# A rewritten opening: two dummies ahead of the data, other line sums, another order of the first steps

## The chip, the cores and the metric

The kernel runs on one core of a Trainium2 chip. The metric is device time in microseconds of one execution. The kernel before takes 1026.65 us (median of 3 runs, 1025.84 to 1027.16).

## The reference

Attention over a pooled key/value image, followed by a gated feed-forward network (FFN). There are 4 images (B), 12288 query rows (N) each, 128 channels (C).

```
kv_pool = kv.reshape(B, 96, 4, 8, 4, C).mean(axis=(2, 4))      # 4x4 pooling: 768 keys
k = v   = kv_pool.reshape(B, 768, C) @ w_sr
a       = softmax(q @ k.T / sqrt(C))
x       = (a @ v).reshape(B * N, C)
out     = (relu(x @ w_gate) * (x @ w_val)) @ w_out             # hidden width 1536
```

Inputs and output are fp32.

## The kernel before, in words

**Tiles.** The 49152 query rows are cut into 96 tiles of 512 rows (`T`). Four tiles are a group (`GRP`) that is loaded together. The 768 keys of an image are six chunks of 128 (`NJC`), the FFN's hidden width is 12 blocks of 128 (`NFB`). For each tile the kernel computes scores, exponentials, the weighted sum x of the values, the FFN's two projections, their gated product and the output projection. The division by the sum of the exponentials is put off to the output, where its square is applied, since the gated product is of second degree in x.

**The order of the work** is written out by hand. Each engine takes its instructions strictly in the order in which the words of a list emit them. A steady tile runs the words of `STEADY`, the last tiles those of `DRAIN` and `LAST`. Ahead of that stands one long list, `OPENING`: it covers the load, pooling and projection of image 0, tiles 0 to 3 through the attention, tiles 0 to 2 through the FFN's projections, the output projections of tiles 0 and 1, and the scores of tiles 4 and 5. A word may carry `@n`, the PSUM bank that its result is to use; a product into a bank waits until the bank's last reader is done.

**The words of OPENING** (the function `open_step` turns them into instructions):

- `Tj.d` turns line d of chunk j: four 128x128 fp32 transposes on TensorE, accumulated in one bank, so that the turn also adds the four pixels of a line (`turn_add`, L280, instructions at L285). A chunk's pooling is a sum over 4 lines of 4 pixels.
- `aj`, `bj`, `cj` add lines of a chunk elementwise on VectorE or GpSimd before any turn (`sum_lines`; `SUMS` says which lines, "s" being the sum so far). `pj` adds the sum's pixels 0,1 to 2,3, and `rj` those two to one (`sum_pixels`). `Tj.p` then turns two blocks, `Tj.r` one block, in place of four for each line.
- `kvTj` copies the turned chunk out of PSUM (`turned`), `pjj` projects it (`project_chunk`, L299), `keyj` keeps the keys, `vtj` transposes them to values (L310), `valj` keeps those.
- `casti` converts a query tile to fp16, `qti` transposes it on TensorE (L205), `qTi` copies it out. For tiles 4 and 5, `qT` is a DMA transpose instead.
- `Sk.j` is the score product of tile k with chunk j (L359), `Ek.j` its exponential on ScalarE (L362), `Vk.j` the product with the values (L437), `xTk` the copy of x. `U` sums the exponentials of chunks with a product by ones (L455), `R` turns those sums into the output's scales.
- `vk.f`, `gk.f`, `ok.f` are the FFN products (L478, L489, L519), `yk.f` copies a v product out of PSUM (by default on ScalarE), `hk.f` multiplies it with the gate on VectorE (L497). `sk.n`, `ek.n` are the scores and exponentials in the steady form.
- `gate`, `W`, `wo`, `ql`, `qd`, `qn`, `tq`, `k` issue DMAs: the FFN's weights, query tiles 4 and 5, the second half of query group 1, later groups.
- `F256` is one dummy product, 256 columns wide.

`ENGINES` names the engine of the words that have a choice (a ScalarE, v VectorE, p GpSimd).

**Loads.** Lines of two chunks are one DMA of 512 KB (`kv_load`, L242). In order of issue on the sync queue, with lines 1 and 3 of the first pair on ScalarE's queue: the four lines of chunks 0 and 1; `w_sr`; query tiles 0 and 1 as one DMA; line 0 of chunks 2 and 3; query tiles 2 and 3; lines 1 to 3 of chunks 2 and 3; the four lines of chunks 4 and 5 (`kv_line`).

**Dummies.** `fill(3)` (L639, instructions at L635) issues three products of 512 columns on the identity matrix before any data is needed. Being fp32, each runs as two passes. They write the bank that the first turn uses next.

Of the kernel before, what the change touches and what calls it, by code (L numbers as in the profile page):

```python
# [9 lines left out]
FP32 = mybir.dt.float32  # L10
# [6 lines left out]
def kernel(  # L17
# [27 lines left out]
    r = 4  # L45
# [18 lines left out]
    assert NFB == 2 * NJC and NST % GRP == 0 and W // r == 8 and HC == 64  # L64

    ENGINES = dict(word.split(":") for word in """
        kvT0:v cast1:a cast0:p kvT1:v key0:v key1:a val0:v qT1:a qT0:v val1:a cast2:v cast3:a
        qT2:v a2:v a3:v p2:v qT3:v b3:p c3:v kvT2:a p3:v key2:a kvT3:a val2:v a5:v a4:v key3:a
        p5:v b4:v r5:v c4:v val3:a kvT5:a p4:v key5:a kvT4:v key4:v val5:a val4:v cast4:p xT2:v
        xT3:v y2.0:v cast5:p y2.3:a y2.1:v y2.2:a y2.5:a y2.6:a xT1:a y2.4:a y1.5:a y1.4:a xT0:a  # L70
        y1.9:a y1.6:a y1.1:a y1.7:a y1.3:a y0.11:a y1.2:a y0.7:v y1.11:a y1.0:a y0.4:a y1.8:a
        y1.10:a y0.2:a y0.8:v y0.5:a y0.10:a y0.0:a y0.3:a y2.11:a y0.9:a y0.1:a y0.6:a y2.8:v
        y2.10:a y2.7:a y2.9:a
    """.split())
    OPENING = """
        T0.1@0 T1.1@1 T0.0 T1.0 F256 T0.3 T0.2 T1.2 kvT0 T1.3 cast1 cast0 pj0@0 kvT1 key0 pj1@1
        vt0@0 qt1@2 key1 val0 qt0@3 qT1 vt1@1 qT0 val1 S1.0@0 S1.1@1 E1.0 S0.1@2 cast2 S0.0@3
        cast3 qt2@4 V1.0@0 qT2 E0.1 qt3@5 a2 S2.1@4 E1.1 S2.0@2 V0.1@6 E2.1 a3 V1.1 E2.0 V2.1@1
        p2 T2.2@4 E0.0 qT3 b3 T2.p S3.0@2 V0.0 E3.0 T2.3 S3.1@3 c3 kvT2 V3.0@2 E3.1 V2.0 pj2@4 p3
        V3.1 key2 T3.p@3 S2.2@4 kvT3 vt2@5 S1.2@7 E2.2 val2 pj3@3 gate2.1 a5 W0 S3.2@5 E1.2 V2.2  # L80
        a4 S0.2@4 key3 E3.2 V1.2 S3.3@3 p5 S2.3@7 E0.2 W1 ql4 ql5 T5.2@5 b4 E3.3 V3.2 vt3@4 V0.2
        r5 E2.3 T5.3 c4 wo val3 T5.r V3.3 kvT5 p4 S0.3@3 pj5@4 E0.3 T4.p@5 S1.3@7 key5 kvT4 V2.3
        E1.3 S3.5@3 pj4@4 E3.5 vt5@5 S2.5@7 key4 V0.3 val5 S2.4@4 E2.5 vt4@3 S3.4@5 val4 V3.5
        E2.4 V2.5 S0.4@3 E3.4 cast4 V2.4 S1.5@4 E0.4 xT2 V1.3 qT4 V3.4 E1.5 S1.4@5 xT3 V0.4 E1.4
        v2.0@1 qd1 v2.3@3 y2.0 v2.1@4 cast5 y2.3 v2.2@2 V1.5 y2.1 g2.0@5 y2.2 qd3 qT5 v2.5@1
        v2.6@3 h2.0 qd0 y2.5 g2.1@2 g2.5@4 V1.4 y2.6 qd2 h2.1 g2.2@1 v2.4@5 xT1 g2.3@3 h2.2
        g2.4@2 y2.4 S0.5@7 h2.3 v1.5@0 E0.5 v1.4@1 v1.9@5 h2.4 g1.5@3 y1.5 V0.5 U0.1.2.3.4.5@7
        h2.5 y1.4 xT0 h1.5 y1.9 v1.6@0 R g1.9@1 y1.6 v1.1@2 v1.7@3 h1.9 g1.7@4 y1.1 v1.3@0 g1.1@5
        tq1 y1.7 s4.0 h1.1 g1.6@1 y1.3 v0.11@2 g1.2@3 e4.0 h1.6 o1.5@5 o1.1 v1.2@0 h1.7 g1.4@1
        y0.11 s4.1 h1.4 y1.2 g1.3@4 v0.7@2 e4.1 o1.6 h1.3 qn1.3 g0.11@0 v1.11@1 o1.4 y0.7 y1.11  # L90
        v1.0@4 o1.3 h0.11 s4.2 y1.0 g1.0@1 e4.2 g1.8@2 h1.2 v0.4@0 v1.8@4 h1.0 o1.9 y0.4 g1.11@3
        s4.3 y1.8 h1.11 o1.0 v0.8@0 e4.3 k5 g0.7@1 h1.8 v1.10@3 o1.2 g0.4@4 h0.7 y1.10 v0.2@2
        o1.7 h0.4 y0.2 o1.11 v0.5@1 g0.10@3 y0.8 y0.5 g1.10@2 o1.8 g0.2@4 h1.10 v0.10@1 v0.0@0
        y0.10 s5.0 h0.2 o0.4@2 y0.0 o1.10 h0.10 g0.8@1 e5.0 v2.11@4 v0.3@0 oT1 o0.10 g0.9@3 y0.3
        o0.11 h0.8 g0.0@5 y2.11 o0.7 h0.0 g0.3@0 v0.9@1 v0.1@4 h0.3 y0.9 s5.1 o0.0 y0.1 v0.6@5
        h0.9 v2.10@0 e5.1 g2.6@1 g0.6@4 h2.6 o0.3 v2.8@3 y0.6 o0.2 y2.8 s5.2 y2.10 g2.9@1 v2.7@5
        h0.6 e5.2 g0.1@3 g2.7@0 o0.8 h0.1 g0.5@4 y2.7 s5.3 h0.5 v2.9@3 e5.3 g2.8@5 o0.9 h2.7
        g2.11@4 o0.5 y2.9 o0.6 h2.8 o0.1 g2.10@0 h2.9 h2.10 h2.11 oT0
    """.split()
    LAST = [f"{head}{n}" for n in range(NFB) for head in "ovygh"] + ["oT"]  # L100
    DRAIN = """
# [42 lines left out]
    def engine_of(name):  # L144
        return {"a": nc.scalar, "v": nc.vector, "p": nc.gpsimd}[ENGINES.get(name, "a")]

    def q_load(g):
        if not 0 <= g < NG:
            return
        b, n0 = divmod(g * GRP * T, N)  # L150
        q16 = work.tile([128, GRP * NS, C], FP16, tag="q16", bufs=2)
        rows = q[b, n0 : n0 + GRP * T, :]
        if g == NG - 1:
            nc.gpsimd.dma_start(q16, rows.rearrange("(p s) c -> p s c", p=128))
        else:
            rows = rows.rearrange("(i t j s) c -> j t i s c", i=GRP, t=32, s=NS)
            for j in range(4):
# [117 lines left out]
    def sum_pixels(name, chunk):  # L275
        s1 = sums.pop(chunk)
        pixels[chunk] = work.tile([128, 2, C], FP32, tag="kv_c2", bufs=2, name="kv_c2")
        add(name, pixels[chunk], s1[:, 0:2], s1[:, 2:4])

    def turn_add(chunk, lines):  # L280
        first = chunk not in kv_Ts
        if first:
            kv_Ts[chunk] = bank([128, 128])
        for i in range(lines.shape[1]):
            nc.tensor.matmul(  # L285
                kv_Ts[chunk], lines[:, i], ident, is_transpose=True,
                start=first and i == 0, stop=False, skip_group_check=True,
            )

    def turned(name, chunk):  # L290
        kvT = work.tile([128, 128], FP32, tag="kvT_chunk", bufs=3, name="kvT_chunk")
        copy_on(name, kvT, freed(kv_Ts[chunk]))
        kv_Ts[chunk] = kvT
# [3 lines left out]
    def project_chunk(jc):
        key_ps[jc] = bank([128, 128])
        nc.tensor.matmul(key_ps[jc], w_sr_f32, kv_Ts.pop(jc), start=True, stop=True)  # L299

    def keep_keys(name, jc):
        pr, engine = freed(key_ps.pop(jc)), engine_of(name)
        if engine is nc.scalar:
            nc.scalar.mul(kv16[:, 0, jc, 0:C], pr, 1.0 / (r * r))
        else:
            engine.tensor_scalar(kv16[:, 0, jc, 0:C], pr, 1.0 / (r * r), None, op0=ALU.mult)

    def turn_chunk_values(jc):
        value_ps[jc] = bank([128, 128], FP16)
        nc.tensor.transpose(value_ps[jc], kv16[:, 0, jc, 0:C], ident16)  # L310

    def keep_chunk_values(name, jc):
        copy_on(name, kv16[:, 0, jc, C : 2 * C], freed(value_ps.pop(jc)))
# [336 lines left out]
    def open_step(word):  # L650
# [59 lines left out]
        elif head == "gate":  # L710
            nc.gpsimd.tensor_copy(gate, line(2 * at[0], at[1])[:, 0, 0:1])
        elif head == "ql":
            q_load_tile(at[0])
        elif head == "wo":
            nc.gpsimd.dma_start(wo16, moe_w_out.rearrange("(fb f) c -> f fb c", f=128))
        elif head == "qd":
            q_tiles(1)
            rows = q[0, GRP * T : 2 * GRP * T, :].rearrange(
                "(i t j s) c -> j t i s c", i=GRP, t=32, s=NS
            )  # L720
            j = at[0]
# [148 lines left out]
```

## Time and profile before

| quantity | value |
|---|---|
| median of 3 runs | 1026.65 us |
| the profiled execution, its own time | 1026.18 us |
| its span in the trace | 1024.4 us |
| TensorE busy | 1017.8 us (99%) |
| ScalarE busy | 919.4 us (90%) |
| VectorE busy | 865.0 us (84%) |
| GpSimd busy | 523.4 us (51%) |
| data moved by DMA | 153.49 MB, mean 150 GB/s |

The profile is one execution on the chip. Its time includes 1.8 us around the span of the trace. A line of the trace's timeline gives the start, the duration, the engine (PE is TensorE's products, PEld its weight loads, DVE VectorE, ACT ScalarE, POOL GpSimd, SP the sync engine), the source line, the operation with output and input, the count of merged instructions, and in brackets the idle time before it with what ended it. Products overlap: the duration of one covers its latency, so the rate is read from start to start. Stretches are given in microseconds from the span's start.

### The profile page before, as it was taken

Reading aid. Unit: us, or ns where it says so; the run is one execution under the profiler, and the core shown is the slowest. Engines: PE = TensorE matmul, PEld = TensorE weight load, DVE = VectorE, ACT = ScalarE, POOL = GpSimd, SP = SyncE. Lnnn points to the kernel's source line nnn. Section 1 sums busy time; section 2 is a strip of 40 time slices with the busy share of each in tenths; the row PEclk is TensorE's granted clock in tenths of the full one; section 3 lists DMA queues with packets and bytes.
Section 4 is the critical chain, followed back from the end, with each engine's and each line's share of the span. In section 5 each row is a group of like instructions: output and inputs, shape, how many; then the busy total and the mean of one; then the engine's idle time right before and its main releaser. Section 6 shows DMA issues by size and latency. Waiting matters only on the chain.

```text
span 1024.4 us, 17497 instructions
## 1 busy us (share of the span) xinstructions
PE 1017.8 (99%) x5039; PEld 488.2 (48%) x5039; DVE 865.0 (84%) x1439; ACT 919.4 (90%) x1929; POOL 523.4 (51%) x1308
## 2 busy tenths in 40 slices
PE   9999999999999999999999999999999999999998
PEld 5444444444444444444444444444444444444445
DVE  3988888888888888888888888888888888888887
ACT  5999999999999999999999999999999999999986
POOL 2587857344347576544434856754334443443342
PEclk9999999999999999999999999999999999999999
DMA  9999999887898998869889899797686986876641
GB/s 318 149 188 158 180 209 145 164 137 126 133 200 156 188 198 152 142 119 144 132 131 199 164 186 206 136 143 134 119 137 105 148 129 119 129 124 115 108 83 42
DMA packets 475312, 153.49 MB, mean 150 GB/s; under 512 B 451536, under 2 KB 465360, under 8 KB 475216
## 3 DMA queue, kind: packets, MB, share of 16 engines
q1 hardware_dynamic: 453184, 126.08, 67.0%
q0 software_dynamic: 21600, 25.19, 16.1%
q10 hardware_dynamic: 432, 1.11, 0.3%
q8 instruction: 40, 0.66, 0.3%
q14 instruction: 56, 0.46, 0.1%
HBM read 53.94 MB, written 26.35 MB: 78 GB/s over the span
## 4 chain that ended last, share of the span: by engine, by line
PE 99%; ACT 0%; issue 0%; POOL 0%; DVE 0%; POOLq 0%
PE bank_ps L489 24%; PE bank_ps L478 24%; PE bank_ps L519 24%; PE wide_ps L378 12%; PE bank_ps L420 12%; PE bank_ps L503 1%; PE bank_ps L285 1%; PE bank_ps L635 1%; PE bank_ps L437 0%; PE bank_ps L359 0%; PE wide_ps L317 0%; ACT aT L362 0%; PE bank_ps L299 0%; PE bank_ps L455 0%; ACT qT L140 0%
## 5 line engine op out<-in xcount | busy, mean ns | idle before, releaser
L497 DVE SCALAR_TENSOR_TENSOR hT<-bank_ps,val 128x512 f16<-128x512 f32 x1152 | 728.0, 679 | 104.0 <-PE bank_ps L489 83.2
L140 ACT CAST val<-bank_ps 128x512 f16<-128x512 f32 x1147 | 628.0, 596 | 44.9 <-PE bank_ps L478 24.9
L478 PE MATMUL bank_ps<-xT,wv 128*128 128x512 f16 x1152 | 419.7, 379 | 0.0
L489 PE MATMUL bank_ps<-xT,wg 128*128 128x512 f16 x1152 | 376.5, 379 | 0.0
L519 PE MATMUL bank_ps<-hT,wo 128*128 128x512 f16 x1116 | 348.2, 379 | 0.0
L383 ACT ACTIVATE a<-wide_ps 128x768 f16<-128x768 f32 x368 | 302.1, 821 | 43.3 <-PE wide_ps L378 43.2
L378 PE MATMUL wide_ps<-kv,qT 128*128 128x512 f16 x736 | 179.7, 326 | 0.0
L420 PE MATMUL bank_ps<-aT,kv 128*128 128x512 f16 x552 | 178.8, 379 | 0.0
L519 PEld LDWEIGHTS <-wo 128*128 128x128 f16 x1116 | 109.2, 98 | 131.6
L489 PEld LDWEIGHTS <-wg 128*128 128x128 f16 x1152 | 112.7, 98 | 122.7
L532 POOL TENSOR_TENSOR o_sb<-o_t,scale 128x512 f32<-128x512 f32 x89 | 93.3, 1049 | 144.7 <-issue 127.2
L478 PEld LDWEIGHTS <-wv 128*128 128x128 f16 x1152 | 112.7, 98 | 105.1 <-issue 0.6
L404 POOL COPY scale<-square 32x8 f32<-32x8 f32 x736 | 141.8, 193 | 28.6
L397 POOL TENSOR_TENSOR square<-inverse 128x8 f32<-128x8 f32 x46 | 9.4, 203 | 256.2 <-DVE inverse L395 249.1
L800 POOL DMA_DIRECT2D out_dram<-o_sb x208 | 130.5, 630 | 16.1 <-POOL o_sb L532 13.0
L378 PEld LDWEIGHTS <-qT 128*128 128x128 f16 x736 | 72.0, 98 | 86.9 <-issue 0.2
L428 DVE CAST xT<-bank_ps 128x512 f16<-128x512 f32 x92 | 63.6, 691 | 32.1 <-PE bank_ps L420 32.1
L420 PEld LDWEIGHTS <-kv 128*128 128x128 f16 x552 | 54.0, 98 | 65.1
L383 ACT ACTIVATION_READ_ACCUMULATOR a<-wide_ps 128x1 f32 x368 | 76.0, 206 | 0.0
L527 DVE STREAM_TRANSPOSE o_t<-bank_ps 128x512 f32<-128x512 f32 x93 | 65.4, 703 | 0.1
L158 POOL DMA_DIRECT2D q<-in_q_dram x84 | 46.7, 572 | 0.6 <-ACT val L140 0.4
L252 POOL TENSOR_TENSOR s<-kv_in 128x512 f32<-128x512 f32 x36 | 45.2, 1284 | 0.7
(83 smaller groups left out, 208.0 us busy)
## 6 DMA issues: line engine op xcount, KB each, us to landing
kv_in<-in_kv_dram SPq DMA_DIRECT2D x42, 512.0 KB, 4.8
out_dram<-o_sb SPq DMA_DIRECT2D x177, 64.0 KB, 3.7
out_dram<-o_sb POOLq DMA_DIRECT2D x176, 64.0 KB, 4.3
q<-in_q_dram POOLq DMA_DIRECT2D x84, 128.0 KB, 6.3
aT<-a SPq DMA_TRANSPOSE x184, 4.6
kv_line<-in_kv_dram SPq DMA_DIRECT2D x4, 512.0 KB, 9.9
placed<-blocks SPq DMA_DIRECT2D x9, 128.0 KB, 2.2
kvT<-placed SPq DMA_DIRECT2D x36, 32.0 KB, 2.0
```

Of the source, the lines that this page charges most:

```text
L140: nc.scalar.copy(to, what)
L378: nc.tensor.matmul(s_ps[:, j0 * 128 : j1 * 128], qT, kv16[:, b, j0:j1, 0:C], start=True, stop=True)
L383: nc.scalar.activation(a16s[k][:, s, :], s_banks.pop(s)[:, 0:J], AF.Exp, scale=qk_scale, accum_out=a_sums[k // 2][:, k % 2, s : s + 1],)
L404: nc.gpsimd.tensor_copy(to[32 * b : 32 * (b + 1), :, :, j], squares[k // 2][32 * j : 32 * (j + 1)])
L420: nc.tensor.matmul(x_banks[k], kv16[:, k // NST, jc, C : 2 * C], aT[:, jc], start=first, stop=x_left[k] == 0,)
L478: nc.tensor.matmul(proj_banks["v", k, fb], wv16[:, fb * 128 : (fb + 1) * 128], xTs[k], start=True, stop=True,)
L489: nc.tensor.matmul(proj_banks["g", k, fb], wg16[:, fb * 128 : (fb + 1) * 128], xTs[k], start=True, stop=True,)
L497: nc.vector.scalar_tensor_tensor(hTs[k][:, fb, :], freed(proj_banks.pop(("g", k, fb))), 0.0, vals.pop((k, fb)), op0=ALU.max, op1=ALU.mult,)
L519: nc.tensor.matmul(o_banks[k], wo16[:, fb, :], hTs[k][:, fb, :], start=first, stop=o_left[k] == 0)
L527: nc.vector.transpose(o_t, freed(o_banks.pop(k)))
L532: nc.gpsimd.tensor_tensor(to, o_by, scale.to_broadcast([128, NS, 4, 32]), op=ALU.mult)
L800: queue.dma_start(*out_moves.pop())
```

## The change

Five edits, all in what runs before the steady list, but for the last:

- `fill(3)` becomes `fill(2)`, and `F256` goes from the list.
- Other line sums. Chunk 1 turns lines 1 and 0 and adds lines 3 and 2 elementwise (`a1`, `p1`, `r1`, then `T1.r`); chunk 3 is turned by lines 3 and 2 and the sum of lines 0 and 1 (before: all four lines summed); chunk 5 has three lines summed (before: two).
- `OPENING` and `ENGINES` are written anew. Tile 0 comes first where tile 1 did; all four early casts are VectorE's; `U` is split in `U0.1` and `U2.3.4.5`; tile 0 goes through the FFN first where tile 2 did; the four `qd` come ahead of `cast4` and `cast5`.
- `turned`, `project_chunk`, `keep_keys`, `turn_chunk_values` and `keep_chunk_values` take a unit that may be a pair of chunks. `PAIRED` is empty, so each unit is one chunk, as before.
- `q_load` takes the parts to load; the last query group is loaded with four DMAs of four row blocks each instead of one DMA.

```
 OPENING (its beginning)
-    T0.1@0 T1.1@1 T0.0 T1.0 F256 T0.3 T0.2 T1.2 kvT0 T1.3 cast1 cast0 pj0@0 kvT1 key0 pj1@1
-    vt0@0 qt1@2 key1 val0 qt0@3 qT1 vt1@1 qT0 val1 S1.0@0 S1.1@1 E1.0 S0.1@2 cast2 S0.0@3
-    cast3 qt2@4 V1.0@0 qT2 E0.1 qt3@5 a2 S2.1@4 E1.1 S2.0@2 V0.1@6 E2.1 a3 V1.1 E2.0 V2.1@1
+    T0.1@0 T1.1@1 T0.0 T1.0 T0.3 a1 T0.2 p1 kvT0 pj0@0 r1 key0 cast0 T1.r vt0@0 cast1 kvT1
+    qt0@2 val0 pj1@1 qT0 qt1@0 key1 cast3 S0.0@2 qT1 vt1@1 cast2 S0.1@3 qt3@4 E0.0 val1
+    S1.1@0 qT3 S1.0@1 E0.1 qt2@5 V0.0@2 E1.1 qT2 S3.1@4 V0.1 E3.1 S3.0@3 a2 S2.1@0 S2.0@5
+    E1.0 V3.1@4 a3 V1.1@6 E2.1 V1.0 T3.2@1 p2 E2.0 p3 T2.2@0 E3.0 r3 V2.0@5 T2.p T3.r T3.3
+    T2.3 kvT3 V2.1 kvT2 pj3@1 pj2@0 key3 V3.0 key2 vt3@1 S2.3@3 val3 S0.3@7 gate2.1 a5 E2.3
+    S0.2@0 S2.2@1 W0 E0.3 a4 V2.3 S3.3@3 E2.2 V0.3 b5 U0.1@7 E3.3 W1 ql4 ql5 S1.3@1 E0.2 b4
+    V3.3 S1.2@3 E1.3 T5.3@0 p5 wo E1.2 c4 T5.p vt2@1 V1.3 kvT5 S3.2@3 val2 p4 pj5@0 E3.2 V0.2
+    key5 T4.p@1 V1.2 kvT4 vt5@0 S0.5@3 val5 pj4@1 E0.5 S2.5@0 key4 V3.2 E2.5 V2.2 S0.4@1
+    vt4@3 V0.5 E0.4 val4 S3.4@0 V2.5 E3.4 S2.4@3 V0.4 S3.5@1 E2.4 xT0 V3.4 S1.4@0 E3.5 V2.4
+    qd2 S1.5@3 E1.4 xT2 v0.3@2 V3.5 qd3 E1.5 v0.9@1 xT3 g0.3@0 qd0 y0.3 v2.1@5 v0.7@3 y2.1
...
-    SUMS = [{}, {}, {"a": [0, 1]}, {"a": [0, 1], "b": ["s", 2], "c": ["s", 3]}, {"a": [0, 1], "b": ["s", 2], "c": ["s", 3]}, {"a": [0, 1]}]
+    SUMS = [{}, {"a": [3, 2]}, {"a": [0, 1]}, {"a": [0, 1]}, {"a": [0, 1], "b": ["s", 2], "c": ["s", 3]}, {"a": [0, 1], "b": ["s", 2]}]
+    PAIRED = ()
...
-    def q_load(g):
+    def q_load(g, parts=range(4)):
...
+        for j in parts:
+            if g == NG - 1:
+                own = slice(j * NS, (j + 1) * NS)
+                nc.gpsimd.dma_start(
+                    q16s[g][:, own], rows.rearrange("(p s) c -> p s c", p=128)[:, own]
+                )
...
-    fill(3)
+    fill(2)
...
-            q_load(3)
+            q_load(3, range(4))
```

The engines of the words around the first steps become: `a1:v p1:v kvT0:a r1:p key0:a cast0:v cast1:v kvT1:a val0:a qT0:v key1:a cast3:v qT1:a cast2:v val1:v qT3:v qT2:v a2:v a3:v p2:v p3:v r3:v kvT3:v kvT2:a key3:a key2:v val3:v`. Of the 36 `y` words of tiles 0 to 2, ScalarE has 33 (before 31) and VectorE 3 (before 5); of the four `xT`, ScalarE has 1 (before 2).

More of the change, by code (lines that the diff above doesn't have):

```diff
@@ L66 @@
     ENGINES = dict(word.split(":") for word in """
[L67 to L71, printed above, removed]
@@ L72 @@
-        y1.10:a y0.2:a y0.8:v y0.5:a y0.10:a y0.0:a y0.3:a y2.11:a y0.9:a y0.1:a y0.6:a y2.8:v
-        y2.10:a y2.7:a y2.9:a
+        a1:v p1:v kvT0:a r1:p key0:a cast0:v cast1:v kvT1:a val0:a qT0:v key1:a cast3:v qT1:a
+        cast2:v val1:v qT3:v qT2:v a2:v a3:v p2:v p3:v r3:v kvT3:v kvT2:a key3:a key2:v val3:v
+        a5:v a4:v b5:v b4:v p5:v c4:v kvT5:a val2:a p4:v key5:v kvT4:a val5:v key4:v val4:v xT0:v
+        xT2:v xT3:v y0.3:a y2.1:v y0.9:a y0.7:a cast4:p y0.0:a y2.0:a cast5:p xT1:a y0.6:a y2.2:a
@@ L74 @@
+        y1.11:a y1.8:a y0.10:a y0.8:a y0.11:a y1.7:a y0.4:a y2.3:a y0.1:a y1.6:a y2.8:a y0.5:a
+        y1.2:a y2.6:a y2.4:a y0.2:a y1.5:v y2.5:a y1.0:a y1.1:a y2.7:v y1.3:a y1.4:a y1.10:a
+        y2.10:a y1.9:a y2.11:a y2.9:a
     """.split())
     OPENING = """
[L76 to L78 removed]
@@ L79 @@
[L79 to L96, printed above, removed]
@@ new lines @@
+        V1.4 y0.9 qd1 v0.0@2 g0.0@4 y0.7 cast4 h0.3 g0.9@1 v2.0@5 y0.0 V1.5 h0.9 qT4 g2.0@3 y2.0
+        v2.2@0 v0.6@2 h0.0 cast5 xT1 g2.1@1 g2.2@5 U2.3.4.5 h2.0 y0.6 qT5 y2.2 h2.1 v1.11@2
+        v1.8@0 h2.2 y1.11 v0.8@1 g1.11@3 R v0.10@4 y1.8 o0.9@2 g0.10@5 y0.10 h1.11 o0.0 v0.11@0
+        y0.8 o0.3 h0.10 g0.8@4 y0.11 v1.7@3 v0.4@1 h0.8 g0.7@5 y1.7 v2.3@0 s4.0 y0.4 v0.1@3 h0.7
+        g0.6@4 e4.0 o0.8 h0.6 g1.8@1 g0.11@5 tq1 o0.7 y2.3 h1.8 o0.10 o0.6 y0.1 g1.7@4 h0.11
+        qn0.11 v1.6@0 g0.4@1 y1.6 v2.8@3 h1.7 g0.1@5 s4.1 y2.8 h0.4 v0.5@0 e4.1 g0.5@4 g2.3@3
@@ L99 @@
+        h1.4 o1.10 g2.10@0 y2.9 o1.9 h2.8 o1.4 s5.3 oT1 g2.9@1 e5.3 h2.9 h2.10 h2.11
     """.split()
@@ L150, in q_load @@
         b, n0 = divmod(g * GRP * T, N)
-        q16 = work.tile([128, GRP * NS, C], FP16, tag="q16", bufs=2)
+        if g not in q16s:
+            q16s[g] = work.tile([128, GRP * NS, C], FP16, tag="q16", bufs=2, name="q16")
         rows = q[b, n0 : n0 + GRP * T, :]
[L153 to L157, printed above, removed]
+        for j in parts:
+            if g == NG - 1:
+                own = slice(j * NS, (j + 1) * NS)
                 nc.gpsimd.dma_start(
-                    q16[32 * j : 32 * (j + 1)].rearrange("t (i s) c -> t i s c", i=GRP), rows[j]
+                    q16s[g][:, own], rows.rearrange("(p s) c -> p s c", p=128)[:, own]
                 )
-        q16s[g] = q16
+            else:
+                nc.gpsimd.dma_start(
+                    q16s[g][32 * j : 32 * (j + 1)].rearrange("t (i s) c -> t i s c", i=GRP),
+                    rows.rearrange("(i t j s) c -> j t i s c", i=GRP, t=32, s=NS)[j],
+                )
     def q_turn_two(g, i):
@@ L278, in sum_pixels, with unit, chunks_of, width @@
         add(name, pixels[chunk], s1[:, 0:2], s1[:, 2:4])
+    def unit(chunk):
+        return NJC + chunk // 2 if chunk // 2 in PAIRED else chunk
+    def chunks_of(u):
+        return slice(2 * (u - NJC), 2 * (u - NJC) + 2) if u >= NJC else slice(u, u + 1)
+    def width(u):
+        return 128 * (2 if u >= NJC else 1)
     def turn_add(chunk, lines):
-        first = chunk not in kv_Ts
+        u = unit(chunk)
+        first = u not in kv_Ts
         if first:
-            kv_Ts[chunk] = bank([128, 128])
+            kv_Ts[u] = bank([128, width(u)])
+        at = 128 * (chunk - chunks_of(u).start)
@@ L284, in turn_add, with turned @@
         for i in range(lines.shape[1]):
             nc.tensor.matmul(
-                kv_Ts[chunk], lines[:, i], ident, is_transpose=True,
+                kv_Ts[u][:, at : at + 128], lines[:, i], ident, is_transpose=True,
                 start=first and i == 0, stop=False, skip_group_check=True,
             )
[L290 to L293, printed above, removed]
+    def turned(name, u):
+        kvT = work.tile([128, 256], FP32, tag="kvT_chunk", bufs=3, name="kvT_chunk")[:, 0 : width(u)]
+        copy_on(name, kvT, freed(kv_Ts[u]))
+        kv_Ts[u] = kvT
@@ L295, with project_chunk, keep_keys @@
     key_ps, value_ps = {}, {}
[L297 to L302, printed above, removed]
+    def project_chunk(u):
+        key_ps[u] = bank([128, width(u)])
+        nc.tensor.matmul(key_ps[u], w_sr_f32, kv_Ts.pop(u), start=True, stop=True)
+    def keep_keys(name, u):
+        pr, engine = freed(key_ps.pop(u)), engine_of(name)
+        pr = pr.rearrange("c (h p) -> c h p", p=128)
+        to = kv16[:, 0, chunks_of(u), 0:C]
@@ L303, in keep_keys @@
         if engine is nc.scalar:
-            nc.scalar.mul(kv16[:, 0, jc, 0:C], pr, 1.0 / (r * r))
+            nc.scalar.mul(to, pr, 1.0 / (r * r))
         else:
[L306 to L313, printed above, removed]
+            engine.tensor_scalar(to, pr, 1.0 / (r * r), None, op0=ALU.mult)
@@ L315, in project, with turn_chunk_values, keep_chunk_values @@
+    def turn_chunk_values(u):
+        own = chunks_of(u)
+        value_ps[u] = bank([128, own.stop - own.start, 128], FP16)
+        for jc in range(own.start, own.stop):
+            nc.tensor.transpose(value_ps[u][:, jc - own.start, :], kv16[:, 0, jc, 0:C], ident16)
+    def keep_chunk_values(name, u):
+        copy_on(name, kv16[:, 0, chunks_of(u), C : 2 * C], freed(value_ps.pop(u)))
     def project(b, pair):
```

8 lines of the change are left out of this document (6 added, 2 removed).

## The prediction

> **What bounds the kernel now.** I read the page first, then busy time by stage, then the opening in order of time (TensorE, then the engines that feed it) with the landings of its loads. All lines are of the kernel before. Page (busy us, share, count) and stages (start:end, length, then busy us of PE, PEld, DVE, ACT, POOL):
>
> ```profile
> PE 1017.8 (99%) x5039; PEld 488.2 (48%) x5039; DVE 865.0 (84%) x1439; ACT 919.4 (90%) x1929; POOL 523.4 (51%) x1308
> ...
> 6.90:12.00 5.10, 4.92 (x40) 4.62 (x41) 0.81 (x3) 0.62 (x1) 0.61 (x1) 1.00 1.03 411
> 12.00:16.00 4.00, 3.51 (x28) 1.80 (x27) 2.66 (x7) 3.58 (x9) 0.00 (x0) 1.00 1.03 410
> 16.00:20.00 4.00, 3.88 (x25) 2.70 (x25) 1.95 (x6) 3.18 (x9) 2.01 (x3) 1.00 1.03 410
> 20.00:25.00 5.00, 5.00 (x31) 2.94 (x32) 3.67 (x9) 4.57 (x12) 2.91 (x7) 1.00 1.08 209
> ...
> 200.00:400.00 200.00, 200.00 (x966) 94.81 (x965) 171.24 (x284) 182.94 (x386) 105.59 (x265) 1.00 0.89 163
> ```
>
> TensorE has no idle time from 20 to 1012 us, so whatever the opening saves or loses on TensorE arrives at the end undiminished. Only the list up to STEADY changes; STEADY, DRAIN and LAST keep their words. The DMA column is near 1 from 7 to 25 us: landings there are set by bytes already queued.
>
> The opening in order of time (start us, duration us):
>
> ```profile
> 1.37 5.49 PE L635 MATMUL bank_ps<-ident 128*128 128x512 f32 x6 [1.37 <-POOL ident masks.py:199]
> 6.92 2.12 PE L285 MATMUL bank_ps<-ident,kv_in 128*128 128x128 f32 x16
> 8.87 0.60 PE L644 MATMUL bank_ps<-ident 128*128 128x256 f32 x2
> 9.31 1.91 PE L285 MATMUL bank_ps<-ident,kv_in 128*128 128x128 f32 x16
> ...
> 13.04 1.02 PE L359 MATMUL bank_ps<-qT,kv 128*128 128x512 f16 x4 [0.35 <-ACT qT L140]
> ```
>
> ```profile
> 10.38 0.62 ACT L140 CAST q<-q 128x512 f16<-128x512 f32 x1 [6.81 <-DMA q<-in_q_dram]
> ```
>
> ```profile
> 12.97 0.42 DVE L142 CAST q<-q 128x512 f16<-128x512 f32 x1
> ```
>
> Landings (issue start plus us to landing), one line for each of three DMAs, issued at 0.74, 4.25 and 11.66:
>
> ```profile
> kv_in<-in_kv_dram ACTq DMA_DIRECT2D x1, 512.0 KB, 4.3
> ...
> q<-in_q_dram SPq DMA_DIRECT2D x1, 512.0 KB, 8.7
> ...
> kv_line<-in_kv_dram SPq DMA_DIRECT2D x1, 512.0 KB, 10.2
> ```
>
> In the same way: first pair of chunks, line 1 at 5.04, line 0 at 6.24, line 3 at 8.53, line 2 at 8.90; q tiles 0 and 1 at 10.38; q tiles 2 and 3 at 12.95; second pair's last two lines at about 15.5 and 16.74; third pair's last line at 11.66+10.2 = 21.86. No edit touches an issue ahead of these, so I keep these times.
>
> **Units, from start to start.** A 512-wide product (S, V, v, g, o) 0.2155 us. A turn of one 128x128 fp32 block 0.1085 us (four to a line). Four q turns 0.215; pj 0.2165; vt 0.054; the 24 products of U 1.41. A dummy's two passes start 0.857 us apart each, two dummies 3.43 us. On ACT an exponential frees its bank after 0.60 and lets the next start after 0.49; a 128-wide copy 0.27. On DVE cast or qT 0.42, line sum 0.68, pixel sum 0.42.
>
> **Part 1, the front.** One dummy goes (2 x 0.857 = 1.71 us) and F256 (8.87 to 9.31, 0.44), together 2.15. What follows decides if it counts. Two dummies end near 5.15, when line 1 is there. Turning at the dummies' half pace, 16 turns x 0.214 = 3.4 us reach 8.6, just when line 3 lands; if the pace rises earlier, TensorE waits for 8.53 instead. T0.3 and T0.2 then end by 9.7, kvT0 9.96, pj0, key0 10.7. Chunk 1's other lines go to DVE (a1 8.93 to 9.61, p1 10.06) and POOL (r1). POOL's price for a 128x128 add is not shown: 0.19 (its 32x8 copy) to 1.38 (its 128x512 add). I take 0.5, nearer the small one; even 1.38 only uses up the wait found next. cast0 waits for q at 10.38 and ends 10.83, qT0 about 11.7, S0.0 at 11.75, S0.1 at 12.03.
>
> **The added wait.** qt3 now stands ahead of S1.1 and S1.0 in TensorE's queue and needs cast3, which can't start before 12.97: qt3 at 12.97+0.42+0.03 = 13.42. Behind it queue S1.1 and S1.0, so E1.1 too, and ACT idles from 13.4 to 14.05; val1, which frees S1.0's bank, stands behind cast3 and cast2 on DVE (+0.07). At 13.47 the kernel before has issued two S (S1.0, S1.1) with chunks 0 and 1, qt0 and qt1 done: the state that the new list has at 13.42. So the 2.15 us of dummies are worth 0.05; q's landing takes the rest.
>
> **Part 2, the turns left.** Before: 55 turns, 32 of them done by then, 23 left. After: 16+9+10+9+2+6 = 52, 25 done, 27 left. Four more x 0.1085 = +0.43 us on the path; a smaller total is no help here.
>
> **Part 3, stalls up to the FFN.** Before, from 13.04 to v2.0 at 28.13 is 15.09 us. Work: 23 S and 21 V 9.48, qt 0.43, 23 turns 2.50, pj 0.87, vt 0.22, sum 13.50; stalls 1.59 (the largest: 0.33 before V2.1 at 16.08, 0.28 before qt3 at 14.61, 0.19 before V3.1 at 18.88). After, laying the words end to end on the three engines with these units: V3.1 15.65, T3.2 16.3, T2.3 ends 18.6, S2.3 19.6, V2.3 20.64, T5.3 22.6 (line there at 21.86, so not late), key5 24.4, V0.5 26.1, v0.3 28.33. Work from 13.42: 22 S and 21 V 9.27, qt 0.43, 27 turns 2.93, pj 0.87, vt 0.22, U0.1 0.47, sum 14.19 of 14.91; stalls 0.72. Bounds for these: 0 to 1.6 (as many as before).
> At v2.0 before has 1 S, 3 V and U's 1.41 to do (2.27); at v0.3 after has 3 V and U's other 0.94 (1.59). Ahead in work 0.69, later by 0.20: **gain 0.49 us**. With the bounds: from a gain of 1.2 to a loss of 0.4.
>
> **Part 4, hidden or even.** From 28 to the end of the list both issue the same v, g, h, y, o and s. Before shows about 0.35 us of gaps on TensorE there; for after I bound 0 to 1 and take the same, since DVE, at 5.00 of 5 from 40 to 45 us, gets two y fewer and one xT more. The four qd issues move ahead of cast4 and cast5 on POOL, so from 30.1 to about 23. They stand behind wo on the same queue, which lands at 30.9. If they slow the others, by 256 KB at that queue's 1.40 MB in 10.8 busy us = 2.0 us, qT4 comes at 35.4 instead of 33.4 and wo at 32.9; s4.0 is reached near 36.2 and the first o near 34.0, so both still hide. cast5 no longer waits behind qd1. Four stores of the last q group in place of one cost POOL three issues x 0.57, hidden by its 49% idle share. **Sum: 1026.18 (profiled execution; span 1024.40) - 0.49 = 1025.7.** That execution lies 0.47 under the median of 1026.65, so against the median 1026.2.
>
> **A row and a rule.** The dummies' passes start 0.857 us apart for 512 columns; F256's take 0.22 for 256, half the time per column. The turns step from 0.26 to 0.11 us near 7.3: there the pace doubles, 5.8 us after the first dummy, and it holds through 32 turns with only F256 between. Whether turns help to raise it the trace can't show, as only two had run.
> The Trainium skill, "TensorE: Matmul & The Clock Gate", Part 1, has the clock double after one busy window of about 3.4 us; Part 4 says transposes don't count as busy in the same way. By Part 4 the two dummies would hardly fill a window; by Part 1 alone the turns complete it, and my sum stands. The rise near 7.3 agrees with Part 1; nothing here shows Part 4.
>
> **Rivals.**
> 1. *The pace stays low (slower).* If turns don't raise it, 3.4 us of dummies, against 5.1 before, are too few. TensorE's work from 13.4 then takes twice as long until a long stretch of plain products: at the earliest the one ending near 18, costing (18-13.4)/2 = 2.3 us, plus 0.3 in the front; if broken off by the turns of chunks 3 and 2, some 5 us. Price 2.3 to 5, less the 0.49: 1028.5 to 1031, most likely 1029. For: no dummy lies between the turns any more. Against: the turns themselves doubled in pace, and three timed runs within 1.3 us look like a clock that comes reliably. It decides from about 5 us of delay in the rise. 17%.
> 2. *The whole front counts.* 2.15 of dummies + 0.33 (three turns fewer) = 2.5 us, 1024.2. It needs q earlier than 12.95, or S work that runs around qt3. Against: TensorE takes its words in order. 7%.
> 3. *A new stall after 28 us*, ACT's or DVE's order, without the low pace: 0.5 to 2.5 slower, 1027.7. For: 33 y on ACT instead of 31. 10%.
>
> **How the numbers follow.** Forecast, the re-laid list with q's landing as its gate: 66%, 1025.0 to 1027.3. About 0.2% (2.05 us) is what a measurement of this kernel can tell from no change. Over that on the fast side: rival 2, 0.07. On the slow side: three quarters of rival 1 (0.13) and four tenths of rival 3 (0.04), 0.17. The rest 0.76. The range leaves out rival 2 and rival 1 above 1029.2: 1024.9 to 1029.2.
>
> **What would show it.** Right: T0.1 at about 5.1, qt3 waiting for DVE's cast until 13.4, v0.3 near 28.3, three turns fewer, no idle TensorE from 30 on. Rival 1: 512-wide products 0.43 apart after 13.4. Rival 2: S1.x issued by 12.3. Rival 3: gaps between 28 and 57 us. Wrong altogether: landings that differ, or gaps after 60 us.

## The result and the profile after

| | before | after |
|---|---|---|
| median of 10 runs | 1025.63 us (1024.80 to 1031.80) | 1030.82 us (1027.77 to 1034.91) |
| ratio after / before | | 1.0038, 95% interval 1.0020 to 1.0056 |
| profiled execution, own time | 1026.18 us | 1030.87 us |
| its span | 1024.4 us | 1029.1 us |

The change makes the kernel slower, by 0.4 to 0.5%: the ratio weighs all runs, that of the two medians is 1.0051. One run of before in the comparisons below, 1057.28 us at a granted clock of 0.96, was in a slow state and is in no count. The page of after, busy time by engine, then from its chain of work the shares of the span:

```profile
PE 1018.9 (99%) x5032; PEld 486.9 (47%) x5032; DVE 867.5 (84%) x1443; ACT 919.3 (89%) x1928; POOL 524.4 (51%) x1310
...
PE 95%; DMA 3%; DVE 1%; issue 0%; SPq 0%; ACT 0%; ACTq 0%
```

TensorE has 7 instructions fewer: two passes of a dummy, two of F256 and three turns, as counted in advance. It is busy 1.1 us longer all the same, and its span is 4.7 us longer: idle time and slower products, not more work. The stages, in the columns and boundaries used for before:

```profile
6.90:12.00 5.10, 3.34 (x26) 2.40 (x25) 2.36 (x5) 0.99 (x4) 0.46 (x1) 1.00 1.04 414
12.00:16.00 4.00, 3.33 (x25) 1.67 (x24) 2.76 (x8) 3.26 (x7) 0.00 (x0) 1.00 1.03 410
16.00:20.00 4.00, 4.00 (x31) 3.25 (x30) 1.70 (x6) 2.23 (x6) 0.45 (x2) 1.00 1.03 410
20.00:25.00 5.00, 4.96 (x34) 2.38 (x32) 4.36 (x10) 4.56 (x10) 5.00 (x11) 1.00 1.08 215
200.00:400.00 200.00, 200.00 (x966) 94.78 (x965) 171.51 (x285) 182.80 (x385) 103.15 (x251) 1.00 0.92 164
```

Up to 25 us TensorE is short of work only ahead of 16 us, and after 200 us both kernels are alike. So I looked between. I followed the loss with one marker: the start of the first score product of each tile, in after less in before, both as profiled.

| first scores of tile | 4 | 5 | 6 | 8 | 12 | 17 | 18 | 95 |
|---|---|---|---|---|---|---|---|---|
| before, us | 35.74 | 45.17 | 54.24 | 75.01 | 116.47 | 169.16 | 179.52 | 980.65 |
| after is later by | 1.66 | 2.60 | 1.42 | 1.37 | 1.91 | 1.96 | 5.83 | 5.82 |

The two jumps are what the prediction had not: 0.5 us between tiles 8 and 12, 3.9 us between 17 and 18. From tile 95 to the end after is 1.15 us shorter than before, as 12 of the 17 other profiled executions are too, before with the front alone changed among them; I don't put that down to the change. 5.82 - 1.15 = 4.67 us; the spans differ by 4.7.

TensorE in after, in order of time (start, duration, in brackets the idle time before and what ended it):

```profile
1.37 3.78 PE L654 MATMUL bank_ps<-ident 128*128 128x512 f32 x4 [1.37 <-POOL ident masks.py:199]
5.35 2.25 PE L300 MATMUL bank_ps<-ident,kv_in 128*128 128x128 f32 x16 [0.20 <-DMA kv_in<-in_kv_dram]
8.92 1.09 PE L300 MATMUL bank_ps<-ident,kv_in 128*128 128x128 f32 x8 [1.32 <-DMA kv_in<-in_kv_dram]
...
13.60 0.40 PE L209 MATMUL bank_ps<-ident,q 128*128 128x128 f16 x4 [0.68 <-DVE q L143]
...
28.98 0.38 PE L497 MATMUL bank_ps<-xT,wv 128*128 128x512 f16 x1
...
55.66 0.48 PE L397 MATMUL wide_ps<-kv,qT 128*128 128x512 f16 x2 [0.56 <-ACT a L402]
...
179.68 0.58 PE L439 MATMUL bank_ps<-aT,kv 128*128 128x512 f16 x1 [2.02 <-DMA aT<-a]
```

The first four lines are the prediction's Part 1: TensorE waits 1.32 us for line 3 and 0.68 us for the cast of q. The 28.98 is v0.3, forecast for 28.33. The last two are losses that the prediction had at nothing. At 55.66 tile 6's scores (s6.0) wait for an exponential; at 179.68 a product waits for the transposed exponentials `aT`, which come by a DMA. The waits of TensorE's products over the whole of after (us in total, times, longest):

```profile
PE bank_ps L439 <- DMA aT<-a: 2.2, 2, 2.0
...
PE wide_ps L397 <- ACT a L402: 0.6, 1, 0.6
```

The 2.0 us grew into 3.9. Windows of 2 us around it, TensorE alone (length, busy us, instructions, granted clock, DMA share, GB/s):

```profile
174.00:176.00 2.00, 2.00 (x12) 1.00 1.33 139
176.00:178.00 2.00, 1.66 (x8) 1.00 1.42 152
178.00:180.00 2.00, 0.32 (x1) 0.92 1.84 199
180.00:182.00 2.00, 2.00 (x7) 0.50 0.86 109
182.00:184.00 2.00, 2.00 (x8) 0.72 1.23 289
```

After the wait the granted clock is 0.50, then 0.72: 7 and 8 products in 2 us where 12 fit. The half clock lasts from 179.70 to 183.11, and half of these 3.41 us is the other 1.7 us. Where the transpose came from, in the chain of work that ended last:

```profile
168.27 0.24 PE bank_ps L439 x2
168.51 11.03 DMA aT<-a
179.54 0.14 issue
179.68 0.58 PE bank_ps L439
```

It was issued at 168.5 and took 11.03 us to land. The sync queue of after, and below it GpSimd's (I read an issue that lasts long as one that the queue holds back):

```profile
43.96 2.81 SPq L246 DMA_DIRECT2D kv_in<-in_kv_dram  x2
47.60 2.82 SPq L429 DMA_TRANSPOSE aT<-a  x1
52.24 5.93 SPq L173 DMA_TRANSPOSE qT<-q  x1
...
166.92 3.79 SPq L429 DMA_TRANSPOSE aT<-a  x2
```

```profile
168.33 2.21 POOL L162 DMA_DIRECT2D q<-in_q_dram  x4
```

The first of the four loads of a query group (128 KB each) starts 0.2 us ahead of the transpose. In before the same pair, and the first product that needs it, stood at

```profile
164.31 3.71 SPq L410 DMA_TRANSPOSE aT<-a  x2
...
175.53 0.38 PE L420 MATMUL bank_ps<-aT,kv 128*128 128x512 f16 x1
```

so two transposes were issued from 164.31, ahead of that kernel's loads at 166.36. The second, issued at 165.90, landed 7.7 us later, 1.9 us ahead of its need. I call this the margin of a tile: from the landing of its last transpose to the start of the first product that needs it.

| margin of tile, us | 4 | 6 | 8 | 10 | 13 | 15 | 17 | least of 17 to 95 |
|---|---|---|---|---|---|---|---|---|
| before | 6.7 | 8.2 | 1.0 | 1.1 | 0.7 | 1.9 | 8.5 | 7.4 |
| after | 2.3 | 3.6 | 0.0 | 0.1 | 0.2 | 0.1 | 9.6 | 7.5 |

So margin is thin up to tile 15, about 180 us, and nowhere later, in both kernels; that is why both are alike from there on. After comes out of the opening with less of it. In the opening before's k5 transpose held the sync queue 2.42 us at 49.55; after's held it 5.93.

### The profile page after: what moved, and what is told of

It is laid out like the page before. It is cut to its first block, busy times and chain, and to the rows that moved or that the text cites. A ratio compares the mean times of both kernels' runs of the same rounds, so it can differ in the third digit from the quotient of the medians.

```text
span 1029.1 us, 17498 instructions
## 1 busy us (share of the span) xinstructions
PE 1018.9 (99%) x5032; PEld 486.9 (47%) x5032; DVE 867.5 (84%) x1443; ACT 919.3 (89%) x1928; POOL 524.4 (51%) x1310
## 4 chain that ended last, share of the span: by engine, by line
PE 95%; DMA 3%; DVE 1%; issue 0%; SPq 0%; ACT 0%; ACTq 0%
PE bank_ps L508 24%; PE bank_ps L497 23%; PE bank_ps L538 23%; PE bank_ps L439 12%; PE wide_ps L397 11%; DMA aT<-a 2%; DMA q<-in_q_dram 1%; PE bank_ps L522 1%; PE bank_ps L456 0%; PE bank_ps L378 0%; DVE hT L516 0%; PE wide_ps L336 0%; PE bank_ps L300 0%; SPq L246 0%; PE bank_ps L314 0%
```

## The experiments

The rivals were: (a) the opening list itself costs the time; (b) transposes of `a` that land late cost it, because query loads are issued in bursts beside them; (c) the low clock of the prediction's rival 1. A late transpose doesn't strike in each execution. So beside medians I count runs over 1029 us: 23 of 146 of before, 12 of 23 of after, over all comparisons. After's opening alone puts it up to 1.4 us later; over 1030.4 us after has 9 of 23. Four profiled executions are over 1029 (after, a_s53, d_after, d_kv), all with a wait of over 1 us that ends as a transpose lands; no long run of before was profiled. The versions ran on several chips, each beside runs of before. After had ten runs in the first comparison, twelve in d_after's and one (a_again) beside a_s53, a_q3late and a_qspread.

**a_again**: after, unchanged.

> The changed kernel once more, unchanged, for a second profile. In the first profile the time went to three places: the opening list up to tile 6's first scores (reached 1.42 us later than before: 55.66 against 54.24), a wait of 0.2 us for a's transpose at 104, and one of 2.0 us at 177.5 with a granted clock of 0.50 to 0.72 in the four us after it (about 1.7 us). Theory Q (the sync queue is behind by a transpose or two from 52 us on, and a transpose misses its product): the opening's 1.4 us comes again within 0.2, waits for a's transposes come again somewhere between 60 and 200 us, at the same or other tiles, and set the rest of 3 us. Theory L (all of it is in the list's order): both come again exactly. Theory C (the clock stays low after two dummies): turns 0.21 us apart after 8 us, which the first profile did not have.

1027.82 us. Tile 6 came 1.14 us late, tile 18 2.53: a wait of 1.1 us at the same place, with no clock loss. The trace names VectorE as its end, but the product starts 0.14 us after its transpose landed, as at 179.68 in after. The opening's part repeats; the later part varies.

**a_s53**: s5.3 and e5.3 earlier in after's list, so that e5.3 is done when s6.0 needs it.

```
- y2.11 h1.9 v2.9@4 g2.8@5 e5.2 g2.11@2 h1.4 o1.10 g2.10@0 y2.9 o1.9 h2.8 o1.4 s5.3 oT1 g2.9@1 e5.3 h2.9
+ e5.2 y2.11 h1.9 v2.9@4 g2.8@5 g2.11@2 h1.4 o1.10 s5.3 g2.10@0 e5.3 y2.9 o1.9 h2.8 o1.4 oT1 g2.9@1 h2.9
```

> The changed kernel with s5.3 and e5.3 eight products earlier, and e5.2 ahead of y2.11, so that tile 6's first scores need not wait for e5.3 (0.56 us idle before them in the changed kernel, 0.72 late). Both theories: s6.0 comes 0.5 to 0.7 us earlier than 55.66. Theory L: the time falls by that, 0.5 to 0.7. Theory Q: by that too if the late transposes stay as they were, but as the margin of a's transposes against their products is under 1 us, the wait near 177 can change by more than the 0.7 us, either way (0 to 4 us of gain, or 1 of loss).

1029.16 us, ratio 1.0021 (1.0006 to 1.0036). A miss. Tile 6 is 1.99 us late, more than in after. Its waits on TensorE:

```profile
PE bank_ps L508 <- ACT val L141: 0.7, 1, 0.7
PE bank_ps L497 <- ACT val L141: 0.6, 1, 0.6
```

The wait for ScalarE's exponential became two for ScalarE's copies of v products, which now stand behind that exponential. ScalarE isn't full there: it idles 1.01 us before e5.3, for the product s5.3. The order on both engines binds, and this reorder moved the wait.

**a_q3late**: query group 3 loaded at tile 7, in place of with k5.

```
-            q_load(3, range(4))        (word k)
+        if k == 7:
+            q_load(3)
```

> The changed kernel with the load of query group 3 (four DMAs, 512 KB of input) issued at the start of tile 7's step in place of the word k5, so not right behind group 2's at 43 to 45 us, where two image lines and a's transposes took 10.3 to 12.1 us to land. Theory Q: the qT transpose of k5 no longer holds the sync queue for 5.9 us, landings at 42 to 50 us fall to 5 to 8, the queue's lag is a transpose shorter, and the waits at 104 and 177 go: 2 to 4 us faster than the changed kernel (1027 to 1029). Theory L: no change over 0.5 us.

1026.87 us, ratio 1.0006 (0.9986 to 1.0027); 2 of 10 runs over 1029. Tile 7 is 1.05 us late, tile 18 1.73.

**a_qspread**: the steady stretch loads one part of a query group in each tile, in place of four in one.

```
-        if ph == 1:
-            q_load(g + 2)
+        if k > 8:
+            q_load(g + 2 if ph else g + 1, [(ph - 1) % 4])
```

> The changed kernel with each later query group (4 to 23) loaded in four parts of 128 KB, one in each of four steps, in place of 512 KB in one step. Theory Q: in the first profile the transpose that was waited for at 177.5 was issued at 168.5, in the same 0.2 us as the four DMAs of a query group, and took 11.0 us to land against 3.8 just before; with one DMA in its place it lands in 4 to 8, so the wait at 177.5 and its low clock go (3 to 4 us of gain), the opening's loss stays (1.4 us): 1026.5 to 1028. Theory L: no change over 0.5 us.

1027.41 us, ratio 1.0001 (0.9987 to 1.0016); none over 1029. Tile 7 is 1.12 us late, tile 18 2.41: waits remain, none listed over 0.5 us.

**a_qboth**: after with both edits.

> The changed kernel with both edits of the query loads: group 3's at tile 7's step, later groups' in four parts over four steps. Alone, the first left tile 18's first scores 1.7 us late against before's profile and the second 2.4, where the changed kernel had 5.8 and 2.5 in two profiles. Theory Q: the wait of tile 17's step (0.69 with the first alone) and the small ones of tiles 8 to 12 (1.1 with the second alone) go both, tile 18's lateness is tile 6's, 1.1: a median of 1026.0 to 1027.0, and no run over 1029. Theory L: as the changed kernel's best, but its spread stays.

1026.64 us (1026.09 to 1027.11), ratio 1.0003 (0.9989 to 1.0018). Lateness is 1.39 us at tile 7 and 1.39 at tile 95: nothing is lost later. How long transposes of `a` took to land from 157 to 176 us, first in after, then in a_qboth:

```profile
DMA to landing us min/median/max: 3.8/4.2/11.0
```

```profile
DMA to landing us min/median/max: 3.7/4.4/6.2
```

The median hardly moves; the worst does. The same holds from 80 to 980 us in all profiles: the longest landing is 10.6 to 12.9 us in the twelve with loads in bursts, before's own among them (12.3), and 7.6 to 9.3 in the seven with loads one to a tile. So bursts make late landings in both kernels; whether one costs time depends on the margin:

| margin of tile, us | 4 | 6 | 8 | 10 | 13 | 15 | 17 |
|---|---|---|---|---|---|---|---|
| a_q3late | 5.8 | 7.8 | 4.0 | 2.7 | 0.6 | 0.1 | 6.5 |
| a_qspread | 0.5 | 1.3 | 0.0 | 0.1 | 0.9 | 3.5 | 9.8 |
| a_qboth | 5.8 | 8.4 | 7.2 | 6.9 | 8.0 | 10.0 | 14.0 |

The first edit restores the margin that the opening leaves, the second takes away the late landings; it needs both. That is (b). What is left of the change is (a), 1.39 us at the marker. By medians a_qboth is 0.48 us over b_qboth, the same edits on before. One piece of (a) is a_qboth's wait of 0.6 us for the exponential ahead of s6.0, as in after.

**b_again**, **b_qboth** and **b_front**: before unchanged; before with both query edits (and after's `q_load`); before with `fill(2)` and without `F256`.

```
-    fill(3)
+    fill(2)          (and F256 out of the list)
```

> The kernel before once more, unchanged, for a second profile of it. Theory Q: no product waits over 0.5 us for a's transpose between 60 and 200 us, tile 6's first scores at 54.24 within 0.2 and tile 18's at 179.52 within 0.5. The last store of the first profile ended the span 3.9 us after the last copy on ACT, that of the changed kernel 2.8 us after; if that is chance in one transfer, this profile may have either.

> The same two edits of the query loads on the kernel before. Theory Q: its runs over 1028 us (3 of 25 so far: 1028.9, 1031.45, 1032.24) are late transposes too, and they go; the rest stays at 1025 to 1026.5, so the median falls by 0 to 0.7 and the spread to under 2 us. Theory L: no change in median or spread.

> The kernel before with the front of the change alone: fill(2) and no F256, everything else as it was. My prediction's step (the front's 2.15 us of dummies are worth 0.05, the landing of q takes the rest): first scores between 12.3 and 13.04, tile 6's first scores 0 to 0.4 us earlier, the time within 0.5 us of the kernel before. Theory F (the dummies are on the path): 2 us faster. Theory C (two dummies leave TensorE at the low clock): turns 0.21 us apart past 8.5 us, 512-wide products 0.43 apart at 13 us, 2 to 5 us slower.

b_again: 1025.58 us, 0.29 us earlier than the first profile at each tile; its least margin is 3.0 us. b_qboth: 1026.16 us, ratio 0.9999 (0.9985 to 1.0013), none over 1029; its profile had a 1.1 us wait for a landing in the opening, and one of 0.4 for a transpose. b_front: 1025.33 us, ratio 1.0004 (0.9982 to 1.0026): its first scores come at 12.28 us (13.04 and 12.74 in the two profiles of before) and tile 6 0.59 us earlier, but 3 of 10 runs are over 1029. Its turns step by 0.11 us once line 3 is there. So (c) falls: two dummies are enough.

**q_dummies**: a_qboth with `fill(3)` and `F256` put back.

> The changed kernel with both query-load edits (1026.64 median, spread 1.0) and the third dummy and F256 put back. My step (q's landing takes what the dummies save): qt3 still at 13.4 to 13.8, tile 6's first scores within 0.3 of 55.6, the time within 0.4 us of 1026.6. Theory F (the front counts): 1 to 2 us slower.

1026.79 us against 1026.64. qt3 starts at 13.36, tile 6 is 1.63 us late (a_qboth 1.43): the 2.15 us of dummies are worth 0.15 to 0.2, if that much is not chance. In before's own list (b_front, b_fq) they are worth 0.3 to 0.7 at the marker.

**q_xT3**: a_qboth with xT3 on ScalarE, so that VectorE has two xT before v0.3's work and not three. **q_s53y**: a_qboth with a_s53's order and y2.9, y2.11 on VectorE.

```
-        xT2:v xT3:v            +        xT2:v xT3:a            (q_xT3)
-        y2.11:a y2.9:a         +        y2.11:v y2.9:v         (q_s53y, with a_s53's order)
```

> The same kernel with tile 3's xT copy on ScalarE in place of VectorE. In the changed kernel VectorE has three xT copies in a row from 28.06 to 30.3 and starts its gated products at 30.86, where before it started at 29.76, and TensorE idles 0.2 us each near 36.2, 36.8 and 37.7. If VectorE's late start makes these gaps: they shrink by 0.3 to 0.6 in all, and so does the time. If ScalarE is as short there: no gain, the same gaps with ScalarE as their releaser.

> The same kernel with s5.3 and e5.3 eight words earlier, e5.2 ahead of y2.11 as in a_s53, and y2.9 and y2.11 moved from ScalarE to VectorE. a_s53 without the last made tile 6 later (1.99 against 1.42 after before's 54.24), with products waiting 0.7 and 0.6 for ScalarE's copies. If ScalarE's load at the list's end is what costs tile 6 its 0.7: first scores of tile 6 at 54.9 to 55.1 and the time 0.5 to 0.7 under 1026.6. If not, as a_qboth or later.

q_xT3: 1026.73 us, no gain; of three gaps near 36 to 38 us (0.2 each) one went. q_s53y: 1026.25 us (1026.09 to 1026.72), 0.39 less than a_qboth. s6.0 starts at 54.78, 0.54 late where after had 1.42, but tile 7 is 1.05 late, because a new wait follows at once:

```profile
54.78 0.49 PE L397 MATMUL wide_ps<-kv,qT 128*128 128x512 f16 x2
...
55.78 0.38 PE L497 MATMUL bank_ps<-xT,wv 128*128 128x512 f16 x1 [0.25 <-DVE o_t L546]
```

This suggests that the end of the new list is bound by ScalarE and VectorE together, not by one word.

**b_fq**: b_front with both query edits.

> The kernel before with the front alone (two dummies, no F256) and both query-load edits. The front alone had seven of ten runs at 1024.4 to 1026.6 and three at 1029.7 to 1031.5. Theory Q: those three are late transposes and go; all runs at 1024.3 to 1026.2, median 0.3 to 1.2 us under the kernel before. Theory L: the runs over 1029 stay.

1025.40 us (1024.42 to 1026.13), ratio 0.9987 (0.9974 to 1.0001), none of 12 runs over 1029, where 7 of the 35 runs of before beside it were. Every tile is 0.67 us earlier. Of the versions with no run over 1029 it has the lowest median, though its interval touches no change.

**c_kv, c_bkv, c_late**: what in the new list makes late transposes more frequent? c_kv is after with two line loads of image 1 (43.96 us above) issued behind k5 and s5.0; c_bkv is before with two such loads issued earlier, among the transposes; c_late is before with `fill(4)`.

```
-  e4.3 k5 g1.0@1 ... oT0 s5.0 y1.1          (c_kv: words L1, L2 load lines 1 and 2;
+  e4.3 k5 L1 g1.0@1 ... oT0 s5.0 L2 y1.1     the o words, which did, leave them out)
```

> After, with lines 1 and 2 of image 1's first pair issued later, behind the transposes of q tiles 8 and 9 (k5) and after s5.0 on the sync queue, in place of about 44 to 47 us. If these two loads, falling among the transposes at 41 to 50 us, are what makes the sync queue run late: k5's transpose is held about 2.5 us instead of 5.9, transposes of a land in at most about 6 us from 157 to 176 us, the wait of step 17 goes, tile 18 stays at +1.4 (first scores against those of before's first profile) and the time is 1026.5 to 1027.2 with few runs above. If it is the q groups alone: still 2 or more late, tile 18 at +2 to +6, 1027.5 to 1031. Tile 6 stays at +1.1 to +1.5 in both, as the list's own stalls are untouched.

> Before, with lines 3 and 0 of image 1's first pair issued earlier on the sync queue, just ahead of the transposes of a's tile 4, second half (about 43 to 45 us), in place of 52.0 and 53.8. If two loads among these transposes make the sync queue late: k5's transpose is held for some 5 us instead of 2.4 and transposes land later from 85 to 176 us, with a wait at step 12 or 17 in the profile or in several of the runs: 1026.5 to 1030 with a wider spread than before. If the loads' place does not matter: like before, 1025.6 to 1026.2, tile lateness constant.

> Before with four dummies in place of three and the list unchanged: everything from the first turn on some 1.4 to 1.7 us later. If lateness alone brought the late transposes of after, tile 18 is 2 to 4 us later than tile 6 and the time 1029 to 1031. If it is the order and the place of what the new list issues: lateness constant from tile 4 to 95, 1027.2 to 1027.8, the spread as before.

c_kv: 1026.96 us, ratio 1.0016 (0.9996 to 1.0037); k5 held the queue 2.20 us, lateness stays 1.2 from tile 12 to 95, but 4 of 12 runs are over 1029 (before beside it: 8 of 29). c_bkv: 1026.55 us, ratio 1.0004 (0.9979 to 1.0029), k5 held 4.35 us and the margins of tiles 8 to 10 fell to 0.2 to 0.4 us, yet 4 of 12 over 1029, hardly more than before's share. c_late, 1026.36 us, tests nothing: its third and fourth dummy ran at the higher pace (all four take 5.20 us, before's three 5.49), and the first scores came at 12.59 us, no later than before's; 3 of 12 runs are over 1029.

**d_after, d_kv**: after and c_kv's kernel on one chip.

> After unchanged, beside the version with the two line loads later and beside before, on one chip. If the new list makes the late transposes more frequent whatever the chip: more than half of the runs over 1029 us, against a sixth to a third of before's, median 1029.5 to 1031. If that share was one chip's: a third or fewer over 1029, median 1027 to 1028.

> After with lines 1 and 2 of image 1's first pair issued behind k5 and s5.0. If the place of these two loads is what makes the late transposes frequent: a third or fewer of the runs over 1029 us, fewer than after's beside it, median 1026.5 to 1027.3. If not: the same share and median as after's beside it.

d_after: 1028.25 us, ratio 1.0019 (1.0000 to 1.0038), 4 of 12 over 1029. d_kv: 1027.05 us, ratio 1.0008 (0.9995 to 1.0021), 2 of 12. A run of d_kv is the shorter in 111 of 144 pairs. So the place of the two loads seems to cost about 1 us of the median; the share over 1029 is not told apart. Both profiled executions were long ones, and show that the late transpose strikes at more than one place. First d_after, then d_kv:

```profile
PE bank_ps L439 <- DMA aT<-a: 3.7, 3, 1.8
```

```profile
PE bank_ps L439 <- DMA aT<-a: 3.4, 1, 3.4
```

In d_after the two long ones end at 105.34 and 180.76 us, in d_kv the one at 106.62. So moving the line loads doesn't end them; spreading the query loads ends the long ones: with a_qspread's edit, no run over 1029 in 72 runs of seven kernels (a_qspread, a_qboth, b_qboth, q_dummies, q_xT3, q_s53y, b_fq), 62 of them on one chip.

## Why the prediction was wrong, by its own steps

It said 1026.2 us and no change; the median is 1030.82, beyond the range.

- **Part 1, right.** qt3 came at 13.60 (forecast 13.42) for the reason given, q's cast. q_dummies prices the front at 0.15 to 0.2 us, forecast 0.05. Rival 2 falls with it.
- **Part 2, right in its count**: the seven missing instructions include its three turns.
- **A row and a rule.** The eight turns at 8.92 take 1.09 us: 8 x 0.1085 = 0.87 and the last one's latency. So the pace had doubled with two dummies and turns alone, and rival 1 falls. Turns also hold the pace: from 5.70 to 9.00 us after's TensorE ran nothing but turns, 1.98 us of them, and the granted clock is 1.00 there and from 9.00 to 12.00. Whether they help to raise it no run shows. When the pace rises varies: the same three dummies take 5.49 us in before and 4.49 in c_bkv. The Trainium skill, "TensorE: Matmul & The Clock Gate", Part 4, by which the full clock doesn't engage for transposes, is not borne out. Its Part 1, by which the clock's window runs freely, agrees with the varying moment.
- **Part 3, mis-sized.** Forecast a gain of 0.49 us; v0.3 at 28.98 makes it a loss: 0.49 - 0.65 = -0.16. Of the 0.65, qt3's later start is 0.18, and 0.47 are stalls: 28.98 - 13.60 less the 14.19 of work is 1.19, forecast 0.72, within its bounds. The start hangs on landings, which differ between executions (line 3: 8.53 forecast, 8.92 here, 8.49 in b_front); T0.3 stood directly on that landing with no work ahead of it.
- **Part 4, "hidden or even", failed.** It took the gaps from 28 to 57 us as equal in both kernels. After has 0.6 us of gaps near 36 to 38 us. VectorE, which was late by then, is the likely cause, not a shown one (q_xT3 took away one gap of three):

```profile
28.06 0.69 DVE L143 CAST xT<-bank_ps 128x512 f16<-128x512 f32 x1 [0.85 <-PE bank_ps L456]
28.96 1.34 DVE L143 CAST xT<-bank_ps 128x512 f16<-128x512 f32 x2 [0.21 <-PE bank_ps L456]
...
30.86 3.74 DVE L516 SCALAR_TENSOR_TENSOR hT<-bank_ps,val 128x512 f16<-128x512 f32 x6
```

  The three xT run in a row and push the first h to 30.86, 1.1 us later than before's 29.76. Then s6.0 waits for e5.3, the last exponential of the list, on ScalarE:

```profile
54.70 0.81 ACT L402 ACTIVATE a<-wide_ps 128x768 f16<-128x768 f32 x1 [0.37 <-PE wide_ps L397]
```

  That is 0.56 us of waiting, 0.72 from start to start; ScalarE itself stood idle 0.37 us for the product s5.3. So the gaps are 0.6 + 0.72 = 1.3 us where the prediction took 0.35 and bounded by 1. This was rival 3 (10%). With Part 3 it turns the gain of 0.49 into a loss of 1.1, of the lateness of 1.37 us at tile 8; in the versions of after that is 0.90 to 1.43 (1.94 in a_s53, 1.58 with all dummies). On its own it would have been about 1027, inside the range. Four "stores" of the last q group are loads; nothing shows that they cost.
- **The step that decided: "whatever the opening saves or loses on TensorE arrives at the end undiminished".** It took the steady stretch to be a fixed length, since TensorE had no idle time in the one profiled execution. That execution had 0.7 to 2.5 us of margin on the transposes of `a` for seven of the tiles 8 to 15, and their landing times ran from 3.6 to 12.3 us. In after one landed too late: a wait of 2.02 us and 1.7 us of half clock. That part of the loss is 4.4 us by the marker (5.82 - 1.42) and 4.2 by the medians of after and a_qboth (1030.82 and 1026.64, not on one chip); with d_after's 1028.25 it is 1.6. In the first comparison it is most of the result. The prediction named "gaps after 60 us" only as what would make it wrong altogether, without a price.

What stays open: why after's margin is so much thinner out of the opening (2.3 us at tile 4 against 6.7). The trace shows its sync queue more loaded at 41 to 58 us, where two line loads, eight query loads and the transposes meet. The four loads of group 3 have part in it: with them at tile 7 that margin is 5.4 to 6.9 us in five profiles, with k5 0.1 to 4.0 in six, and 6.3 in c_kv. c_bkv, which puts the line loads there in before, lowered it to 4.4 without more long runs; moving them in after took about 1 us from the median. The size varied too: the same kernel stood at a ratio of 1.0038 in the first comparison and 1.0019 in d_after's.

## What to carry to other kernels

"No idle time" in one profile is not "margin": for each wait that is hidden, read how long before its need the data landed, and at how many places that is under the spread of the landings, above all right behind an opening. A change of an opening can then act hundreds of instructions later, through queues that it leaves fuller. Spread a burst of loads that shares the DMA engines with transfers on the path, before tuning the order of words.

## What was not expected of the hardware

- A wait of 2.02 us in after lowered the granted clock to 0.50 for the following 3.41 us, so the wait cost nearly double; a wait of 3.45 us in d_kv did the same for 3.41 us. Waits of 1.63 and 1.83 us in d_after left it at 1.00. The Trainium skill, "TensorE: Matmul & The Clock Gate", section "Why this matters for your kernels", warns of gaps over about 3 us. Here 2.02 us was enough, once.
- A DMA transpose that lands in 4.2 us in the median took 11.03 when issued with four query loads; none took over 6.2 in the same stretch (157 to 176 us) when the loads came one to a tile, nor over 8.0 from 80 to 980 us.
